# All projection products of a two-layer-kind network as 64x32 tiles

## The chip, the cores and the metric

The kernel runs on one core of one Trainium2 chip. The metric is the time of one execution on the device in microseconds (us), as the median of several runs. The core's engines are TensorE (PE in the profile; its weight loads are listed apart as PEld), VectorE (DVE), ScalarE (ACT), GpSimd (POOL) and SyncE (SP). Each takes its own stream of instructions in order; they wait for one another by semaphores.

## The reference

The input x has 2048 tokens of 448 features in bfloat16. Four layers follow one another, A, B, A, B, each added to x after a layer norm of its input; both A layers have the same weights, and so have both B layers.

```python
def A(x, wqkv, wo):        # 16 heads of 28 features
    q, k, v = split(x @ wqkv)
    idx = pos[:, None] - 2 * arange(8)[None, :]      # 8 keys, 2 tokens apart
    logits = einsum("bhsd,bhswd->bhsw", q, k[idx]) * 28 ** -0.5   # masked where idx < 0
    o = einsum("bhsw,bhswd->bhsd", softmax(logits), v[idx])
    return o @ wo

def B(x, w_gate, w_up, w_down):                      # inner size 1792
    return ((x @ w_gate) * (x @ w_up)) @ w_down
...
x = x + A(layernorm(x), A_wqkv, A_wo)
x = x + B(layernorm(x), B_w_gate, B_w_up, B_w_down)
x = x + A(layernorm(x), A_wqkv, A_wo)
x = x + B(layernorm(x), B_w_gate, B_w_up, B_w_down)
```

The matrix products with a weight (queries, keys, values, `wo`, gate, up, down) are called projections below. The two einsums of A are the score products and the value products.

## The kernel before

**Storage.** x stays in SBUF for the whole kernel (`x_sb`). Each layer norm writes normalised blocks of 128 tokens (`xn_sb`), which are transposed into `xnTa` (for A) or `xnTb` (for B), by the DMA queues or, for the first chunks, by TensorE with an identity (line 660). 448 features are 7 times 64, so all projections contract over 64 rows at a time.

**Projections.** Two products of 64 rows and 128 output columns make a pair: one stands on rows 0 to 63 of the array, the other on rows 64 to 127, and they write different PSUM banks. This tile mode is `MAIN = "R64"`. There are three places. `twin` (line 698) computes queries and keys, or the values of two blocks of queries, in 7 pairs, of which 3 come before a crossing and 4 after. At the crossing the two row halves change places: a bank that was written from the upper rows is now written from the lower ones, and TensorE waits for a semaphore of its own earlier products. `twin_blocks` (line 714) computes the product with `wo` and the product with `w_down` for two blocks of 128 tokens, with such a crossing in the middle; the splitting at crossings is made by `crossed`. `b_chunk` (line 983) computes gate (rows 0 to 63) and up (rows 64 to 127), 7 pairs for 128 of the 1792 inner columns, up to 512 tokens long. ScalarE copies gate out of PSUM (line 989), VectorE multiplies it with up (line 992).

**Attention.** Queries are taken in blocks of 120 (128 for the first), two blocks to a group. `attn_front` makes 64 score products of 28 rows by 64 columns (line 862, mode `R32`, placed by `tile_position`), ScalarE exponentiates them (line 869), VectorE masks them (line 879). `attn_back` makes 64 value products of 64 rows by 32 columns (line 896, mode `C32`): eight tiles, two row halves by four strips of 32 columns. Their result is copied into the ring `O_sb` of four slots (lines 910 and 914) and normalised by `norm` (lines 924 to 937). 17 groups' worth of such work, 1088 score and 1088 value products, lie in the two A layers. The last blocks of the last B layer use full-height products of 128 by 128 (line 1004, mode `F`, as are the warm-up of line 565 and the transposes).

**What sets the order.** The kernel writes its instructions into a planner first (`Sched`). Every task has a duration, dependencies, a priority (from its place in `SEQ`, plus the tables `PR` by kind and `JP` by chunk) and, on TensorE, a tile mode; the planner simulates the engines, adds a cost where TensorE changes its mode (`SWITCH`), hands out the 8 PSUM banks (`A_CAP` and `B_CAP` limit what A and B tasks hold while the other waits), and holds tasks of another mode back for a while to collect them (`HOLD_A`, `HOLD_N`). A task of the mode `MAIN` is taken without such holding. The order that comes out is emitted as fixed instruction streams, with semaphore waits where a task depends on another engine. In the estimate of a TensorE task, `n = 2 * len(ins)` is its number of instructions, since every product brings its own weight load:

```python
n = 2 * len(op.ins)
credit = min(self.CREDIT, credit + (now - clast) / self.FETCH)
if n > 40:
    est = max(est, (n - credit) * self.FETCH + (self.HICCUP if n > credit + 40 else 0.0))
```

Of the kernel before, what the change touches and what calls it, by code (L numbers as in the profile page):

```python
# [9 lines left out]
S = 2048  # L10
D = 448
H = 16
# [12 lines left out]
FC = F // 128  # L25
ACT_TABLE_SET = 6

MAIN = "R64"
PE_T = ("00", "01", "02", "03", "04")
HEAD_LN = 5  # L30
HEAD_P = (-53.71, -30.23, -20.33, -12.94, -19.33)
HOLD_A = 1000.0
HOLD_BA = 2000.0
HOLD_BB = 500.0
# [1 line left out]
S_EST = 270.0  # L36
VX = 120.0
# [5 lines left out]
VT = 4  # L43
NV2 = 6
NXN_ = 6
NO = 4
# [2 lines left out]
AVC = True  # L49
AVC_E = ("act", "dve")  # L50
NBK = 8
PR = {'AV': 8.84, 'rstd': -5.66, 'bn': 0.73, 'N': -2.82, 'Gps': -1.08, 'Tps': 16.85, 'H': 18.16, 'S': 10.61, 'VT': 19.61, 'Ex': 16.77, 'G': -2.93, 'xn': -6.19, 'QK': -6.56, 'Ddps': -26.52, 'V': 22.93, 'x': -0.84, 'lnv': -15.5, 'Oc': -6.51, 'Oa': -6.47, 'R': -19.3, 'VVps': 1.22, 'Yps': -25.3, 'PW': 58.69, 'T': -9.57, 'mv': 2.02, 'Rs': -2.57, 'Rl': 21.52, 'QKps': 4.71, 'E': -7.15, 'wqk': -9.31, 'wqp': -11.53}
JP = {'A20': -3.02, 'B32': 16.28, 'B34': 16.21, 'A22': 20.13, 'B13': 2.73, 'A21': 6.27, 'B12': -2.81, 'A02': -0.21, 'A03': 4.03, 'B30': 4.3, 'B31': 8.23, 'B10': 21.86, 'B11': -14.15, 'A23': 29.86, 'A04': -0.79, 'B33': 153.62, 'A01': -5.33, 'B14': 4.53, 'A00': -24.6}
XL = (2300.0, 2200.0, 4200.0, 5000.0, 5500.0)
WVL = 5000.0
STL = (2400.0, 2600.0, 2900.0, 2800.0)
# [8 lines left out]
FILL = 30  # L65
SEED = 190
JITTER = 0
ATT_P = 1.96
A_CAP = 4
B_CAP = 8  # L70
SEQ = "A00 A01 B10 A02 B11 A03 A04 B12 A20 B13 A21 B14 B30 A22 B31 A23 B32 B33 B34".split()


# [38 lines left out]

class Op:
    __slots__ = ("engs", "ins", "est", "deps", "mode", "prio", "acquire", "release", "idx", "eng",
                 "dma", "lat", "after", "start", "end", "seen", "selfd", "tmin")

    def __init__(self, **kw):
        for k in self.__slots__:
# [11 lines left out]
class Sched:  # L130
# [87 lines left out]
    def schedule(self):  # L218
# [5 lines left out]
        mode = None  # L224
        credit, clast = self.CREDIT, 0.0
        ndep, users = {}, {}
        pend = {e: [] for e in self.ENGS}
# [4 lines left out]
        for op in self.ops:  # L232
            srcs = set()
            for k in op.deps:
                src = self.ready[k][0]
                srcs |= {src.idx} if src.dma is None else {o.idx for o in self.dgroup[(src.dma, src.mode)]}
            if op.after is not None:
                srcs.add(op.after.idx)
            ndep[op.idx] = len(srcs)
            for s in srcs:  # L240
                users.setdefault(s, []).append(op)
            if not srcs:
                for e in op.engs:
                    pend[e].append(op)
        left = len(self.ops)
        now = 0.0
        while left:
            moved = False
            b_ready = any(o.acquire is not None and o.acquire.kind == 1 for o in pend["pe"])
            for e in self.ENGS:  # L250
# [2 lines left out]
                best = None  # L253
                cands = []
                for op in pend[e]:
                    r = self.ready_at(op, e)
                    if r <= now + 1e-6:
                        cands.append((op.prio, op.idx, op))
                cands.sort()
                a_wait = False  # L260
# [1 line left out]
                for *_, op in cands:  # L262
                    if op.acquire is not None:
# [4 lines left out]
                        kind = op.acquire.kind  # L268
# [32 lines left out]
                op = best  # L301
# [13 lines left out]
                if e == "pe":  # L315
                    if mode is not None and op.mode != mode:
                        est += self.SWITCH
                    mode = op.mode
                    n = 2 * len(op.ins)
                    credit = min(self.CREDIT, credit + (now - clast) / self.FETCH)  # L320
                    if n > 40:
                        est = max(est, (n - credit) * self.FETCH + (self.HICCUP if n > credit + 40 else 0.0))
                    credit = max(0.0, credit + est / self.FETCH - n)
                    clast = now + est
                op.start, op.end = now, now + est
# [12 lines left out]
                for u in users.get(op.idx, ()):  # L338
                    ndep[u.idx] -= 1
                    if ndep[u.idx] == 0:  # L340
                        for x in u.engs:
                            pend[x].append(u)
            if moved:
# [2 lines left out]
            for e in self.ENGS:  # L346
                if not pend[e]:
                    continue
                if free[e] > now + 1e-6:
                    c = [free[e]]  # L350
                else:
                    c = [self.ready_at(op, e) for op in pend[e]]
                    c += [f + self.LAT for f in self.free_at]
                c = [t for t in c if t > now + 1e-6]
                if c and (nxt is None or min(c) < nxt):
                    nxt = min(c)
# [65 lines left out]

def pe_cols(n):
    return n / 2.4 + 2.6


def act_est(n, psum=True):
# [11 lines left out]
def build(nc, A_x, A_wqkv, A_wo, B_w_gate, B_w_up, B_w_down, out):  # L439
# [42 lines left out]
    sc = Sched()  # L482
# [122 lines left out]
    def ring(n, freekey):  # L605
        i = rpos[n] % len(rings[n])
        rpos[n] += 1
        prev = rings[n][i]
        rings[n][i] = freekey
        return i, prev  # L610
# [63 lines left out]
    def crossed(parts, deps, prio, est, acquire, kind):  # L674
        prev, prevk = None, []
        prio += PR.get(kind, 0.0)
        for n, (half, ins, pdeps) in enumerate(parts):
            cross = n > 0 and half != parts[n - 1][0]
            if n + 1 < len(parts) and parts[n + 1][0] != half:
                xid[0] += 1  # L680
                tags = [("cross", xid[0], h) for h in (0, 1)]
                ins = ins[:-2] + [(fn, [t] + ([k] if k is not None else [])) for (fn, k), t in zip(ins[-2:], tags)]
                nextk = tags
            else:
                nextk = []
            prev = sc.add("pe", ins, len(ins) / 2 * est + (VX if kind == "VVps" else 0.0), deps=deps + pdeps, mode=MAIN, prio=prio, acquire=acquire if n == 0 else None,
                          after=prev, selfd=prevk if cross else ())
            prevk = nextk
        return prev

    def twin(u, tdeps, prio):
        seen, last = set(), {w: (s, h) for s, sl in enumerate(SLOTS) for h, (w, c, lo) in enumerate(sl)}
        parts = [(0, [], []), (1, [], [])]
        for s, sl in enumerate(SLOTS):
            for h, (w, c, lo) in enumerate(sl):
                st, sp_ = w not in seen, last[w] == (s, h)
                seen.add(w)
                parts[0 if s < 3 else 1][1].append((lambda E, w=w, c=c, lo=lo, st=st, sp_=sp_: E.matmul(  # L698
                    u["out"](w), u["lhs"](w, c, lo, lo + 64), u["rhs"](w, c, lo, lo + 64), start=st, stop=sp_), u["keys"][w] if sp_ else None))
        crossed(parts, u["deps"] + tdeps, prio, pe_cols(u["n"]), u["bk"], u["kind"])  # L700

    def twin_blocks(outs, lhs, rhs, keys, groups, gdeps, deps, prio, acquire):
        first, last = groups[0][0], groups[-1][-1]
        parts = []
        for flip in (0, 1):
            for g, chunks in enumerate(groups):
                ins = []
                for c in chunks:
                    for h in (0, 1):
                        w = h ^ flip  # L710
                        st = c == first and flip == 0
                        sp_ = c == last and flip == 1
                        lo = 64 * h
                        ins.append((lambda E, w=w, c=c, lo=lo, st=st, sp_=sp_: E.matmul(outs(w), lhs(w, c, lo), rhs(w, c, lo), start=st, stop=sp_), keys[w] if sp_ else None))  # L714
                parts.append((flip, ins, gdeps[g]))
        crossed(parts, deps, prio, pe_cols(D), acquire, keys[0][0] + "ps")

# [169 lines left out]
    def attn_back(li, g, slot, prio):  # L887
        qbs, nc = grp_qbs(g), grp_nc(g)
        nd = len(qbs)
        bk = Banks(2, pair=True)  # L890
        ins = []
        for hc, d, c, b in [(hc, d, c, b) for hc in range(4) for d in range(nd) for c in range(2) for b in range(4)]:
            h, o, q = 4 * hc + b, (hc * nd + d) * nc, (li, qbs[d])
# [2 lines left out]
            ins.append((lambda E, b=b, c=c, o=o, vw=vw: E.matmul(ps[32 * b:32 * b + 32, bk[c], o:o + nc], vw, E_sb[64 * c:64 * c + 64, slot, b, o:o + nc],  # L896
                                                               start=True, stop=True, tile_position=(64 * c, 32 * b)), None))
        ins[-1] = (ins[-1][0], [("AV", li, q) for q in qbs])
        sc.add("pe", ins, S_EST * nd / 2, deps=[("E", li, g, 0), ("E", li, g, 1), "c_v"] + [(k, li, q) for k in ("V", "VT") for q in qbs], mode="C32", acquire=bk, prio=prio)
        while nd == 2 and rpos["o"] % NO == NO - 1:  # L900
            rpos["o"] += 1
        oring = [ring("o", ("N", li, q)) for q in qbs]
        o0, nq = oring[0][0], qb_info(qbs[0])[3]
        assert nd == 1 or oring[1][0] == o0 + 1
        O = O_sb[:, o0:o0 + nd, 0:4 * nq].rearrange("p d (h n) -> p d h n", h=4)
# [57 lines left out]
    def b_chunk(li, j, n_b, prio):  # L963
# [15 lines left out]
        for m in range(FC):  # L979
            u, ins = us[m], []  # L980
            for k in range(7):
                for w in range(2):
                    ins.append((lambda E, u=u, k=k, w=w: E.matmul(u["out"](w), WGU[64 * w:64 * w + 64, k, 128 * u["fc"]:128 * u["fc"] + 128],  # L983
                                                                 X[64 * w:64 * w + 64, k, c0:c0 + nt], start=k == 0, stop=k == 6), u["keys"][w] if k == 6 else None))
            sc.add("pe", ins, 7 * pe_cols(nt), deps=u["deps"] + tdeps, mode=MAIN, prio=prio, acquire=u["bk"])
            for u in us[m:m + 1]:
                bk, fc = u["bk"], u["fc"]
# [147 lines left out]
```

## Time and profile before

| what | value |
|---|---|
| median of 3 runs | 393.48 us (393.34 to 393.48) |
| span of the profiled execution | 391.9 us |
| around the span (median less span) | 1.6 us |
| instructions in the trace | 13,910 |
| DMA, mean over the span | 57 GB/s |
| DMA in the first three fortieths of the span | 275, 295 and 306 GB/s |

The span runs from the first to the last instruction of the profiled execution; its own time outside the profiler is not listed, so the median stands for it. The page gives busy time by engine, busy tenths in 40 slices, DMA queues, the chain of work that ended last, and the costliest groups of instructions with their mean duration and the idle time before them. [...] The queues of kind "instruction" bring the engines' own instruction streams; the others move data. "issue" as the end of an idle time means that the engine waited for nothing that the profile shows.

### The profile page before, as it was taken

How to read it: one execution, taken by the hardware profiler on the slowest of the kernel's cores; microseconds unless marked ns; L12 is line 12 of the kernel's file. 1: busy time of each engine (PE TensorE's matmuls, PEld its weight loads, DVE VectorE, ACT ScalarE, POOL GpSimd, SP SyncE). 2: the span in 40 equal slices, each digit the busy share in tenths (PEclk: the TensorE clock that was granted, in tenths of full speed). 3: DMA queues.
4: the chain of work that ended last, by engine and by line, in shares of the span. 5: the costliest groups of instructions: out<-in, count | busy, mean ns of one | idle time of the engine just before them, and what ended most of it. 6: DMA issues, size and time to landing. Idle time of an engine off the chain costs nothing.

```text
span 391.9 us, 13910 instructions
## 1 busy us (share of the span) xinstructions
PE 384.9 (98%) x6142; PEld 213.8 (55%) x6142; DVE 271.2 (69%) x596; ACT 207.3 (53%) x398; POOL 7.6 (2%) x36
## 2 busy tenths in 40 slices
PE   8999999999999999999999999999999999999997
PEld 6655657545444544554546867444454544444674
DVE  6989899669967765684788645258942689477252
ACT  4888876478523745467651523268315782263230
POOL 6010000000000000000000000000000000000000
DMA  8990161501220401320121141010050102403101
GB/s 275 295 306 19 24 93 28 106 13 30 48 49 15 80 15 35 64 28 15 17 49 21 36 95 29 25 20 11 12 128 7 26 7 47 95 4 16 34 27 47
DMA packets 54703, 22.47 MB, mean 57 GB/s; under 512 B 44836, under 2 KB 54644, under 8 KB 54644
## 3 DMA queue, kind: packets, MB, share of 16 engines
q1 hardware_dynamic: 53284, 19.47, 23.7%
q10 hardware_dynamic: 1360, 2.12, 1.8%
q8 instruction: 48, 0.79, 0.8%
q14 instruction: 11, 0.09, 0.1%
HBM read 8.54 MB, written 2.71 MB: 29 GB/s over the span
## 4 chain that ended last, share of the span: by engine, by line
PE 90%; DVE 4%; DMA 2%; ACT 2%; issue 1%; SPq 0%; DVEq 0%
PE ps L983 41%; PE ps L714 25%; PE ps L698 16%; PE ps L896 3%; PE ps L862 3%; PE ps L1004 1%; DMA xnTb<-xn_sb 1%; DMA x_sb<-in_A_x_dram 1%; PE ps L660 1%; DVE xn_sb L651 1%; DVE st L630 1%; DVE x_sb L954 1%; ACT R_sb L925 1%; ACT R_sb L926 1%; DVE E_sb L879 0%
## 5 line engine op out<-in xcount | busy, mean ns | idle before, releaser
L983 PE MATMUL ps<-xnTb,WGU 64*128 64x512 bf16 (+1 forms) x1960 | 180.5, 333 | 0.9 <-DMA xnTb<-xn_sb 0.9
L983 PEld LDWEIGHTS ps<-xnTb,WGU 64*128 64x128 bf16 x1960 | 93.5, 94 | 73.8 <-ACT g_sb L989 1.5
L989 ACT ACTIVATE g_sb<-ps 128x512 bf16<-128x512 f32 (+1 forms) x140 | 71.4, 511 | 95.0 <-PE ps L983 94.3
L992 DVE TENSOR_TENSOR hT<-g_sb,ps 128x512 bf16<-128x512 bf16 (+1 forms) x140 | 79.3, 574 | 55.1 <-ACT g_sb L989 46.1
L714 PE MATMUL ps<-WD,hT 64*128 64x448 bf16 x840 | 84.0, 349 | 0.1
L714 PEld LDWEIGHTS ps<-WD,hT 64*128 64x128 bf16 x840 | 40.2, 94 | 37.0 <-DVE hT L992 0.8
L698 PE MATMUL ps<-xnTa,WQK 64*128 64x512 bf16 (+1 forms) x504 | 53.5, 353 | 0.3
L954 DVE TENSOR_TENSOR x_sb<-x_sb,ps 128x448 bf16<-128x448 bf16 x62 | 36.2, 614 | 24.9 <-PE ps L714 24.8
L630 DVE BATCH_NORM_STATS2 st<-x_sb 128x6 f32<-128x448 bf16 x64 | 37.5, 615 | 2.7 <-DMA x_sb<-in_A_x_dram 2.7
L869 ACT ACTIVATE E_sb<-ps 128x1024 bf16<-128x1024 f32 (+1 forms) x36 | 33.5, 980 | 9.6 <-PE ps L862 9.3
L750 ACT ACTIVATE qk<-ps 128x1024 bf16<-128x1024 f32 (+1 forms) x30 | 27.1, 921 | 19.3 <-PE ps L698 19.0
L651 DVE TENSOR_SCALAR xn_sb<-x_sb,mv,rstd 128x512 bf16<-128x512 bf16 (+1 forms) x64 | 33.7, 569 | 4.7 <-ACT rstd L635 4.5
L698 PEld LDWEIGHTS ps<-xnTa,WQK 64*128 64x128 bf16 x504 | 23.5, 94 | 24.0 <-ACT xnTa L666 0.8
L879 DVE TENSOR_TENSOR E_sb<-E_sb,MK 128x1024 bf16<-128x1024 bf16 (+2 forms) x40 | 23.9, 613 | 8.8 <-ACT E_sb L869 8.5
L714 PE MATMUL ps<-wo_g,oT 64*128 64x448 bf16 x256 | 29.1, 349 | 0.0
L633 ACT ACTIVATE lnv<-mv,eps_sb 128x2 f32<-128x2 f32 (+1 forms) x33 | 9.5, 293 | 30.4 <-DVE mv L632 30.2
L937 DVE TENSOR_TENSOR oT<-O_sb,R_sb 128x480 bf16<-128x480 f32 (+3 forms) x36 | 22.1, 627 | 3.4 <-ACT R_sb L926 3.1
L925 ACT ACTIVATE R_sb<-R_sb 128x480 f32<-128x480 f32 (+1 forms) x34 | 20.1, 600 | 5.6 <-DVE R_sb L924 5.6
L924 DVE STREAM_SHUFFLE R_sb<-O_sb 128x480 f32<-128x480 f32 (+1 forms) x34 | 22.7, 696 | 0.0
L698 PE MATMUL ps<-WV,xnTa 64*128 64x336 bf16 (+3 forms) x252 | 22.2, 304 | 0.2
L926 ACT ACTIVATE R_sb<-R_sb 128x480 f32<-128x480 f32 (+1 forms) x34 | 20.1, 602 | 0.4
L714 PEld LDWEIGHTS ps<-wo_g,oT 64*128 64x128 bf16 x256 | 12.3, 94 | 11.6 <-DVE oT L937 0.4
(47 smaller groups left out, 170.7 us busy)
## 6 DMA issues: line engine op xcount, KB each, us to landing
out_dram<-x_sb SPq DMA_DIRECT2D x15, 112.0 KB, 1.7
WD<-in_B_w_down_dram SPq DMA_DIRECT2D x2, 784.0 KB, 11.5
WGU<-in_B_w_up_dram SPq DMA_DIRECT2D x2, 784.0 KB, 17.6
WGU<-in_B_w_gate_dram ACTq DMA_DIRECT2D x2, 784.0 KB, 13.3
x_sb<-in_A_x_dram SPq DMA_DIRECT2D x3, 448.0 KB, 6.4
vt<-qk SPq DMA_DIRECT2D x42, 16.0 KB
xnTb<-xn_sb SPq DMA_TRANSPOSE x32, 3.0
x_sb<-in_A_x_dram SPq DMA_DIRECT2D x2, 224.0 KB, 4.2
```

The costliest lines, as they stand in the source:

```text
L630: sc.add("dve", one(lambda E, B=B: E.bn_stats(st6[:, B, :], x_sb[:, B, :]), ("bn", li, B)), 525.0, deps=[("x", li - 1, B)] + ([("xn", li - ...
L651: sc.add("dve", one(lambda E, B=B, dst=dst, src=src: E.tensor_scalar(dst, src, mv[:, B, 0:1], rstd[:, B:B + 1], ALU.subtract, ALU.mult), ( ...
L698: parts[0 if s < 3 else 1][1].append((lambda E, w=w, c=c, lo=lo, st=st, sp_=sp_: E.matmul(u["out"](w), u["lhs"](w, c, lo, lo + 64), u["rhs ...
L714: ins.append((lambda E, w=w, c=c, lo=lo, st=st, sp_=sp_: E.matmul(outs(w), lhs(w, c, lo), rhs(w, c, lo), start=st, stop=sp_), keys[w] if s ...
L750: return E.activation(dst, src, ACT.Copy) if hasattr(E, "activation") else E.tensor_copy(dst, src)
L869: return E.activation(E_sb[:, slot, 2 * hp:2 * hp + 2, 0:w], ps[:, b0:b0 + 2, 0:w], ACT.Exp, scale=SCALE)
L925: sc.add("act", one(lambda E: E.activation(R_sb[:, rs, 0:w], R_sb[:, rs, 0:w], ACT.Ln), ("Rl", li, qb)), act_est(w, False), deps=[("Rs", l ...
L926: sc.add("act", one(lambda E: E.activation(R_sb[:, rs, 0:w], R_sb[:, rs, 0:w], ACT.Exp, scale=-1.0), ("R", li, qb)), act_est(w, False), de ...
L954: sc.add("dve", one(lambda E: E.tensor_tensor(x_sb[:, B, :], x_sb[:, B, :], ps[:, bk[w], 0:D], ALU.add), ("x", li, B)), dve_est(D), deps=[ ...
L983: ins.append((lambda E, u=u, k=k, w=w: E.matmul(u["out"](w), WGU[64 * w:64 * w + 64, k, 128 * u["fc"]:128 * u["fc"] + 128], X[64 * w:64 * ...
L989: sc.add("act", one(lambda E, gs=gs, bk=bk: E.activation(g_sb[:, gs, 0:nt], ps[:, bk[0], 0:nt], ACT.Copy), ("G", li, j, fc)), act_est(nt), ...
L992: sc.add("dve", one(lambda E, gs=gs, bk=bk, fc=fc: E.tensor_tensor(hT[:, fc, hs, 0:nt], g_sb[:, gs, 0:nt], ps[:, bk[1], 0:nt], ALU.mult), ...
```

## The change

Every projection product of 64 by 128 is written as four products of 64 by 32, one on each strip of 32 array columns, by a new helper:

```diff
-MAIN = "R64"
+MAIN = "C32"
...
-ATT_P = 1.96
+ATT_P = 1.0
 A_CAP = 4
-B_CAP = 8
+B_CAP = 6
...
+def strips(out, lhs, rhs, start, stop, row, key=None):
+
+    def strip(s):
+        return lambda E: E.matmul(out()[32 * s:32 * s + 32], lhs()[:, 32 * s:32 * s + 32], rhs(), start=start, stop=stop, tile_position=(row, 32 * s))
+    return [(strip(s), key if s == 3 else None) for s in range(4)]
```

`twin`, `twin_blocks` and `b_chunk` call it in place of one `E.matmul` each, with `row` 0 or 64:

```diff
-                    ins.append((lambda E, u=u, k=k, w=w: E.matmul(u["out"](w), WGU[64 * w:64 * w + 64, k, 128 * u["fc"]:128 * u["fc"] + 128],
-                                                                 X[64 * w:64 * w + 64, k, c0:c0 + nt], start=k == 0, stop=k == 6), u["keys"][w] if k == 6 else None))
+                    ins += strips(lambda u=u, w=w: u["out"](w), lambda u=u, k=k, w=w: WGU[64 * w:64 * w + 64, k, 128 * u["fc"]:128 * u["fc"] + 128],
+                                  lambda k=k, w=w: X[64 * w:64 * w + 64, k, c0:c0 + nt], k == 0, k == 6, 64 * w, u["keys"][w] if k == 6 else None)
```

So the mode of the projections is that of the value products, and the planner treats the value products as `MAIN` too. The task durations in the planner stay what they were (`len(ins) / 8 * est` in place of `len(ins) / 2 * est`). At a crossing the second half waits for the last product of the first half alone, where there were two tags. In `attn_back` the value products themselves now wait for a free slot of `O_sb`, where only the copies did:

```diff
-        sc.add("pe", ins, S_EST * nd / 2, deps=[("E", li, g, 0), ("E", li, g, 1), "c_v"] + [(k, li, q) for k in ("V", "VT") for q in qbs], mode="C32", acquire=bk, prio=prio)
+        sc.add("pe", ins, S_EST * nd / 2, deps=[("E", li, g, 0), ("E", li, g, 1), "c_v"] + [(k, li, q) for k in ("V", "VT") for q in qbs] + [r[1] for r in oring], mode=MAIN, acquire=bk, prio=prio)
```

The planner's estimate for a task with many instructions becomes

```diff
-                    if n > 40:
-                        est = max(est, (n - credit) * self.FETCH + (self.HICCUP if n > credit + 40 else 0.0))
+                    fetch = (n - credit) * self.FETCH
+                    if fetch > est:
+                        est = fetch + (self.HICCUP if n > credit + 100 else 0.0)
```

The tables `PR`, `JP` and `HEAD_P` have new values, so the order on every engine is another; the rest of the planner's edits (`rdy`) keep a value that was computed anew each time. TensorE's products are 6142 before and 17,578 after.

More of the change, by code (lines that the diff above doesn't have):

```diff
@@ L26 @@
 ACT_TABLE_SET = 6
-MAIN = "R64"
+MAIN = "C32"
 PE_T = ("00", "01", "02", "03", "04")
 HEAD_LN = 5
-HEAD_P = (-53.71, -30.23, -20.33, -12.94, -19.33)
+HEAD_P = (-60.1, -28.46, -20.04, -19.66, -19.03)
 HOLD_A = 1000.0
@@ L51 @@
 NBK = 8
-PR = {'AV': 8.84, 'rstd': -5.66, 'bn': 0.73, 'N': -2.82, 'Gps': -1.08, 'Tps': 16.85, 'H': 18.16, 'S': 10.61, 'VT': 19.61, 'Ex': 16.77, 'G': -2.93, 'xn': -6.19, 'QK': -6.56, 'Ddps': -26.52, 'V': 22.93, 'x': -0.84, 'lnv': -15.5, 'Oc': -6.51, 'Oa': -6.47, 'R': -19.3, 'VVps': 1.22, 'Yps': -25.3, 'PW': 58.69, 'T': -9.57, 'mv': 2.02, 'Rs': -2.57, 'Rl': 21.52, 'QKps': 4.71, 'E': -7.15, 'wqk': -9.31, 'wqp': -11.53}
-JP = {'A20': -3.02, 'B32': 16.28, 'B34': 16.21, 'A22': 20.13, 'B13': 2.73, 'A21': 6.27, 'B12': -2.81, 'A02': -0.21, 'A03': 4.03, 'B30': 4.3, 'B31': 8.23, 'B10': 21.86, 'B11': -14.15, 'A23': 29.86, 'A04': -0.79, 'B33': 153.62, 'A01': -5.33, 'B14': 4.53, 'A00': -24.6}
+PR = {'AV': -76.5, 'rstd': 11.09, 'bn': 0.91, 'N': 7.02, 'Gps': -1.64, 'Tps': 7.27, 'H': -12.07, 'S': 4.41, 'VT': -10.04, 'Ex': 17.97, 'G': 87.98, 'xn': -12.63, 'QK': 3.17, 'Ddps': -20.99, 'V': 31.96, 'x': -0.65, 'lnv': -11.9, 'Oc': -7.3, 'Oa': -5.3, 'R': -21.09, 'VVps': 2.07, 'Yps': -57.58, 'PW': 44.14, 'T': -2.37, 'mv': -4.13, 'Rs': -11.6, 'Rl': 26.4, 'QKps': 4.71, 'E': -5.63, 'wqk': -9.37, 'wqp': -8.95}
+JP = {'A20': -39.71, 'B32': 34.27, 'B34': -54.93, 'A22': 20.53, 'B13': 4.2, 'A21': 15.6, 'B12': -0.24, 'A02': 1.24, 'A03': 9.63, 'B30': 6.56, 'B31': 7.4, 'B10': -7.36, 'B11': -26.26, 'A23': 30.63, 'A04': -58.23, 'B33': 7.56, 'A01': -4.1, 'B14': 3.5, 'A00': -14.21}
 XL = (2300.0, 2200.0, 4200.0, 5000.0, 5500.0)
@@ L114 @@
     __slots__ = ("engs", "ins", "est", "deps", "mode", "prio", "acquire", "release", "idx", "eng",
-                 "dma", "lat", "after", "start", "end", "seen", "selfd", "tmin")
+                 "dma", "lat", "after", "start", "end", "seen", "selfd", "tmin", "rdy")
     def __init__(self, **kw):
@@ L242, in schedule @@
             if not srcs:
+                op.rdy = {x: self.ready_at(op, x) for x in op.engs}
                 for e in op.engs:
@@ L255, in schedule @@
                 for op in pend[e]:
-                    r = self.ready_at(op, e)
-                    if r <= now + 1e-6:
+                    if op.rdy[e] <= now + 1e-6:
                         cands.append((op.prio, op.idx, op))
@@ L340, in schedule @@
                     if ndep[u.idx] == 0:
+                        u.rdy = {x: self.ready_at(u, x) for x in u.engs}
                         for x in u.engs:
@@ L351, in schedule @@
                 else:
-                    c = [self.ready_at(op, e) for op in pend[e]]
+                    c = [op.rdy[e] for op in pend[e]]
                     c += [f + self.LAT for f in self.free_at]
@@ L680, in crossed @@
                 xid[0] += 1
-                tags = [("cross", xid[0], h) for h in (0, 1)]
-                ins = ins[:-2] + [(fn, [t] + ([k] if k is not None else [])) for (fn, k), t in zip(ins[-2:], tags)]
-                nextk = tags
+                tag = ("cross", xid[0])
+                fn, k = ins[-1]
+                ins = ins[:-1] + [(fn, [tag] + ([k] if k is not None else []))]
+                nextk = [tag]
             else:
                 nextk = []
-            prev = sc.add("pe", ins, len(ins) / 2 * est + (VX if kind == "VVps" else 0.0), deps=deps + pdeps, mode=MAIN, prio=prio, acquire=acquire if n == 0 else None,
+            prev = sc.add("pe", ins, len(ins) / 8 * est + (VX if kind == "VVps" else 0.0), deps=deps + pdeps, mode=MAIN, prio=prio, acquire=acquire if n == 0 else None,
                           after=prev, selfd=prevk if cross else ())
@@ L697, in twin @@
                 seen.add(w)
-                parts[0 if s < 3 else 1][1].append((lambda E, w=w, c=c, lo=lo, st=st, sp_=sp_: E.matmul(
-                    u["out"](w), u["lhs"](w, c, lo, lo + 64), u["rhs"](w, c, lo, lo + 64), start=st, stop=sp_), u["keys"][w] if sp_ else None))
+                parts[0 if s < 3 else 1][1].extend(strips(lambda w=w: u["out"](w), lambda w=w, c=c, lo=lo: u["lhs"](w, c, lo, lo + 64),
+                                                          lambda w=w, c=c, lo=lo: u["rhs"](w, c, lo, lo + 64), st, sp_, lo, u["keys"][w] if sp_ else None))
         crossed(parts, u["deps"] + tdeps, prio, pe_cols(u["n"]), u["bk"], u["kind"])
@@ L713, in twin_blocks @@
                         lo = 64 * h
-                        ins.append((lambda E, w=w, c=c, lo=lo, st=st, sp_=sp_: E.matmul(outs(w), lhs(w, c, lo), rhs(w, c, lo), start=st, stop=sp_), keys[w] if sp_ else None))
+                        ins += strips(lambda w=w: outs(w), lambda w=w, c=c, lo=lo: lhs(w, c, lo), lambda w=w, c=c, lo=lo: rhs(w, c, lo), st, sp_, lo, keys[w] if sp_ else None)
                 parts.append((flip, ins, gdeps[g]))
@@ L890, in attn_back @@
         bk = Banks(2, pair=True)
+        while nd == 2 and rpos["o"] % NO == NO - 1:
+            rpos["o"] += 1
+        oring = [ring("o", ("N", li, q)) for q in qbs]
         ins = []
@@ L898, in attn_back @@
         ins[-1] = (ins[-1][0], [("AV", li, q) for q in qbs])
-        sc.add("pe", ins, S_EST * nd / 2, deps=[("E", li, g, 0), ("E", li, g, 1), "c_v"] + [(k, li, q) for k in ("V", "VT") for q in qbs], mode="C32", acquire=bk, prio=prio)
-        while nd == 2 and rpos["o"] % NO == NO - 1:
-            rpos["o"] += 1
-        oring = [ring("o", ("N", li, q)) for q in qbs]
+        sc.add("pe", ins, S_EST * nd / 2, deps=[("E", li, g, 0), ("E", li, g, 1), "c_v"] + [(k, li, q) for k in ("V", "VT") for q in qbs] + [r[1] for r in oring], mode=MAIN, acquire=bk, prio=prio)
         o0, nq = oring[0][0], qb_info(qbs[0])[3]
```

## The prediction

> **What bounds the kernel now.** I read the page's first section, then the chain of waits, then the costliest groups. The profiled execution has a span of 391.9 us; the median of the timed runs is 393.48, so 1.6 us lie around the span and are added at the end.
>
> ```profile
> span 391.9 us, 13910 instructions
> ...
> PE 384.9 (98%) x6142; PEld 213.8 (55%) x6142; DVE 271.2 (69%) x596; ACT 207.3 (53%) x398; POOL 7.6 (2%) x36
> ...
> q8 instruction: 48, 0.79, 0.8%
> ...
> PE 90%; DVE 4%; DMA 2%; ACT 2%; issue 1%; SPq 0%; DVEq 0%
> ...
> L983 PE MATMUL ps<-xnTb,WGU 64*128 64x512 bf16 (+1 forms) x1960 | 180.5, 333 | 0.9 <-DMA xnTb<-xn_sb 0.9
> ```
>
> TensorE is the bound: 98% busy, 90% of the chain. Its work is projection products in pairs, one on rows 0-63 and one on rows 64-127, which run side by side. In the chain 14 such products of 512 columns (7 pairs) take 1.51 us, 216 ns a pair. The third line is the one to keep: q8 is the queue that brings TensorE's instructions, 0.79 MB in 48 refills of 16 KB. TensorE has 12,422 records in the trace (6142 products, 6142 weight loads, 138 waits and the like), 259 for each refill; the stalls below make it 256.
>
> **The array time of a projection does not change.** A pair becomes eight products of 64x32. Attention's value products (line 896) already run in this tile mode, so the trace shows what eight strips do. In the first 0.1 us of the run at 82.45 us, the instructions had piled up ahead of the array, and eight products of 64 columns start every 29 ns (single starts at 82.489, 82.518, 82.547): 64 columns at the full clock (26.7) plus 2.4 ns. The same rule gives 216 ns at 512 columns, what a pair takes now. That the four strips do not run at once is thereby excluded. Nor do weight loads show: the load for the first strip's third product started at 82.502 while its second ran from 82.489. [...]
>
> **What it removes.** I counted mode changes in the two orders of TensorE's instructions: 75 before, 54 after, 21 fewer (value products join the projections; score products, transposes and the last full-height products still switch).
>
> ```profile
> 82.45 0.68 PE L896 MATMUL ps<-E_sb,v_sb 64*32 64x64 bf16 x64
> 83.06 1.69 PE L983 MATMUL ps<-xnTb,WGU 64*128 64x512 bf16 x14
> 84.68 0.71 PE L862 MATMUL ps<-qk 28*64 28x64 bf16 x64
> ...
> 86.78 0.54 PE L896 MATMUL ps<-E_sb,v_sb 64*32 64x64 bf16 x47
> 88.09 0.26 PE L896 MATMUL ps<-E_sb,v_sb 64*32 64x64 bf16 x17 [0.78 <-issue]
> ```
>
> The 14 products from 83.06 take to 84.68, 1.62 us against 1.51 undisturbed: 0.11 for a switch, and other switches lie at 0.09 to 0.11. 21 x 0.10 = 2.1 us off. The second tag of a row crossing is dropped as well; its wait has other work in front of it, so I count nothing.
>
> **What it adds: instructions.** Lines 983, 714 and 698 hold 1960 + 840 + 256 + 504 + 252 = 3812 products. They become 15,248, each with its own weight load: 2 x 11,436 = 22,872 instructions more, 35,294 in all, 22,872 / 256 = 89 refills more, 137 in all. Issue alone has room: in the steady part of line 896 one instruction takes 4.2 ns (8.3 ns a product), so the 16 of an eight-strip group need 67 ns, under the 72 to 216 ns that the group occupies the array. The question is whether the refills keep up.
>
> **What a refill costs.** The last two rows above are a stall: 47 products, nothing from 87.12 to 88.09, then 17. No semaphore ends it; the profile writes "issue". There are two more, at 31.45 (0.15 us) and here:
>
> ```profile
> 266.72 1.34 PE L896 MATMUL ps<-E_sb,v_sb 64*32 64x64 bf16 x126
> 268.24 0.20 PE L896 MATMUL ps<-E_sb,v_sb 64*32 64x64 bf16 x2 [0.17 <-issue]
> ```
>
> Their positions give the cause. Counts of products and weight loads up to just inside each stall:
>
> ```profile
> 0.00:31.50 31.50, 29.01 (x473) 18.03 (x473) 25.73 (x73) 22.90 (x50) 7.62 (x36) 1.00 0.94 278
> 0.00:87.50 87.50, 83.69 (x1741) 51.40 (x1741) 73.55 (x183) 62.46 (x124) 7.62 (x36) 1.00 0.52 130
> 0.00:268.00 268.00, 263.61 (x4528) 149.29 (x4529) 196.56 (x448) 155.92 (x302) 7.62 (x36) 1.00 0.30 67
> ```
>
> With the 15, 39 and 96 other records these are 961, 3521 and 9153 instructions: 2560 and 5632 apart, 10 and 22 times 256 exactly. So each stall stands at a refill boundary. By the trace's packet records the last refill before each was number 3 (28.99 to 30.21 us), 13 (85.64 to 86.70) and 35 (265.82 to 266.90), again 10 and 22 apart. TensorE went on 1.39, 1.39 and 1.34 us after the packet's end. And the next refill was not asked for until then: it started 1.69, 1.99 and 1.34 us after TensorE went on, and took 0.95 us each time. So one refill is in flight at a time, a boundary is not passed until the one before has landed, and the full turn is request + packet + delivery:
> 1.69 + 0.95 + 1.36 = 4.0; 1.99 + 0.95 + 1.36 = 4.3; 1.34 + 0.95 + 1.36 = 3.64 us. Mean 3.98 us for 256 instructions, 15.5 ns each.
>
> Now, 256 instructions last 391.9 / 48 = 8.2 us on average, so only bursts meet that limit. After the change the array wants 256 of them in 16 groups: 3.45 us at 512 columns, 3.0 at 448, 1.75 at 256. Over all projections the array time is 588 x 215.8 + 392 x 109.2 (line 983), 548 x 189.2 (714) and 66.6 (698), 340 us, for 30,496 instructions: 2.85 us per 256. Every kind is under 3.98. So TensorE starves at nearly every boundary, and refills become the bound through the whole kernel.
>
> [...]
>
> **The sum.** TensorE starts projecting at 9.5 us as before and passes the first boundary soon after. The first refills lie in the stretch full of loads: before, number 1 ran 15.46 to 16.59, delivered 17.9; number 3 started 3.6 us after its boundary, so a turn there is 3.6 + 1.2 + 1.36 = 6.2. Refills 2 and 3 land at 24.1 and 30.3, 4 at 34.3 (a turn of 4.0). Then 132 turns to number 136: 132 x 3.98 = 525.4. The last 285 instructions hold the full-height products, slower than a refill:
>
> ```profile
> 381.24 2.75 PE ps L1004 x14
> 383.99 2.76 PE ps L714 x28
> 386.75 2.80 PE ps L1004 x28
> ```
>
> 8.3 us, and 2.35 from there to the end of the span. 34.3 + 525.4 + 8.3 + 2.35 = 570.4, with 1.6 around it **572 us**.
>
> Everything else hides beneath: the 2.1 us of switches, the new order's priorities and bank caps, and the wait that value products now make for a free slot of O_sb (behind it on TensorE's queue stand the next projections, which starve anyway; without that cover it is late by at most one normalisation step, about 0.6 us in rows 924 to 937, 18 times). VectorE and ScalarE, 271 and 207 us busy, get slack.
>
> The unknown is the turn under steady starving. From below: the shortest request that can be read with no stall, about 0.96 us (refill 34, started 259.21, its boundary passed near 258.25), packet 0.95, delivery 1.24 (refill 2, 24.24 to 25.48): 3.15, which gives 462. From above, 1.99 + 1.25 + 1.39 = 4.63: 658. Both ends need the extreme of three terms at once, 133 times; I take the mean of the three turns seen whole, and 475 to 630 as the range (3.25 to 4.4).
>
> **Rivals.**
> - *Refills do not bind* (faster). The buffer holds more blocks than I read, and the three stalls were a late request only. Then the switches count: 393.5 - 2.1, with one long stall (0.97) perhaps gone, **390 to 391.5**. For it: most boundaries in the trace pass without a gap. Against it: those were 5 us and more apart, but for those bursts. It decides if TensorE passes two boundaries within 3 us in a row without stopping.
> - *Two refills in flight.* A block every 2 us: only 256-column stretches starve, (392 + 56) groups x 16 / 256 = 28 blocks x 0.25 = 7, less 2: **398**. Against it: no request went out during the stall of 0.97 us.
> - *Weight loads show* in long columns, 14 ns (load 82.475 to product 82.489) on each of 1906 groups: 27 us, **418**, refills hidden. Against it: the burst above.
>
> **Chances.** Forecast 0.86, refills not binding 0.08, two in flight 0.03, weight loads 0.03. About 0.2% (0.8 us) is what a measurement of this kernel can tell from no change; of the first rival 0.01 falls inside. Faster 0.07, same 0.01, slower 0.92. The range 475 to 630 holds nearly all of the forecast's 0.86, some 0.8.
>
> **What would show it.** In the profile after: q8 with about 137 refills; TensorE's busy share well below 98%, about 60 to 75%, with idle before lines of projections put down to "issue"; stops every 256 instructions and refills 3.6 to 4.3 us apart; groups of eight still 216 ns apart between stops; 54 mode changes. Wrong would be: refills closer than 3 us, or groups slower than 216 ns. If the idle time also lowered the granted clock (1.00 in every window here), it would be slower still.

## The result, and the profile after

The changed kernel takes 550.47 us (three runs, 549.35 to 552.98) where the kernel before takes 393.48: a ratio of 1.4005, 95% interval 1.3944 to 1.4065. The forecast was 572 with a range of 475 to 630. The profiled execution has a span of 551.2 us and took 552.98.

From the page of the changed kernel (sections 1 to 5; PEclk is the granted TensorE clock in tenths for 40 equal slices):

```profile
span 551.2 us, 36763 instructions
...
PE 423.3 (77%) x17578; PEld 267.4 (49%) x17578; DVE 282.8 (51%) x606; ACT 204.4 (37%) x390; POOL 6.8 (1%) x34
...
PEclk9669899999999999999999899999999999999998
...
q8 instruction: 138, 2.26, 1.8%
...
PE 76%; issue 22%; POOL 1%; ACT 1%; DVE 0%; POOLq 0%
...
L432 PE MATMUL ps<-xnTb,WGU 64*32 64x512 bf16 (+1 forms) x7840 | 204.3, 338 | 62.6 <-issue 60.9
```

TensorE falls from 98% busy to 77%, and what replaces it in the chain is not another engine but "issue", from 1% to 22%: TensorE waits for nothing that the profile shows. The instruction queue q8 brings 138 refills in place of 48. The last line is gate and up: 62.6 us of idle time in front of its products, 60.9 of them "issue", where line 983 had 0.9 in all.

The timeline of TensorE in the changed kernel, in a stretch of gate and up at 256 columns (start, length, what, and the idle time before):

```profile
308.29 2.84 PE L432 MATMUL ps<-xnTb,WGU 64*32 64x256 bf16 x128 [2.12 <-issue]
311.76 2.31 PE L432 MATMUL ps<-xnTb,WGU 64*32 64x256 bf16 x127 [0.63 <-issue]
315.65 1.94 PE L432 MATMUL ps<-xnTb,WGU 64*32 64x256 bf16 x128 [1.58 <-issue]
319.00 1.26 PE L432 MATMUL ps<-xnTb,WGU 64*32 64x256 bf16 x73 [1.41 <-issue]
```

This is the whole result in four lines. 128 products with their weight loads are 256 instructions; TensorE does them in 2 to 3 us, stops, and starts again 3.47, 3.89 and 3.35 us after the start before. The second line has one product fewer; waits are instructions of the same stream and count too (the one remainder of 193 below comes out only with them).

Over the whole trace I took the refill packets and the positions in TensorE's stream. A boundary is the place behind a block of 256 instructions; a stop is the time from the last start before it to the first start behind it. Of the 137 boundaries, 129 have a stop of 0.25 us or more, 163.8 us in all. Every one of the 129 stands at a position that leaves 193 when it is divided by 256, as the three stops of the kernel before do (961, 3521, 9153). The span grew by 159.3 us, so the stops account for the loss; the 4.5 us between the two sums were not taken apart. After each stop TensorE goes on 1.2 to 1.7 us after the end of a refill packet, 1.39 on average. No two refills start less than 3.2 us apart. Between the stops a group of eight strips follows the last at 216 ns for 512 columns, 189 for 448 and 109 for 256 (medians, from start to start; a strip of 512 columns is listed with 377 ns, so listed durations overlap), exactly as a pair did.

### The profile page after: what moved, and what is told of

It is laid out like the page before. It is cut to its first block, busy times and chain, and to the rows that moved or that the text cites. A ratio compares the mean times of both kernels' runs of the same rounds, so it can differ in the third digit from the quotient of the medians.

```text
span 551.2 us, 36763 instructions
## 1 busy us (share of the span) xinstructions
PE 423.3 (77%) x17578; PEld 267.4 (49%) x17578; DVE 282.8 (51%) x606; ACT 204.4 (37%) x390; POOL 6.8 (1%) x34
## 4 chain that ended last, share of the span: by engine, by line
PE 76%; issue 22%; POOL 1%; ACT 1%; DVE 0%; POOLq 0%
PE ps L432 69%; PE ps L872 2%; PE ps L909 2%; PE ps L1014 1%; PE ps L669 1%; POOL hT L554 1%; PE ps L574 0%; ACT qk L760 0%; ACT g_sb L999 0%; POOL MK L558 0%; DVE WQK L582 0%; ACT R_sb L936 0%; POOL WQK L545 0%; ACT O_sb L920 0%; DVE hT L1002 0%
## 5 line engine op out<-in xcount | busy, mean ns | idle before, releaser
L432 PE MATMUL ps<-xnTb,WGU 64*32 64x512 bf16 (+1 forms) x7840 | 204.3, 338 | 62.6 <-issue 60.9
L432 PEld LDWEIGHTS ps<-xnTb,WGU 64*32 64x32 bf16 x7840 | 117.9, 93 | 129.9 <-issue 86.9
L432 PE MATMUL ps<-WD,hT 64*32 64x448 bf16 x3360 | 91.7, 352 | 13.3 <-issue 13.3
L432 PEld LDWEIGHTS ps<-WD,hT 64*32 64x32 bf16 x3360 | 52.6, 93 | 43.7 <-issue 21.4
L432 PE MATMUL ps<-xnTa,WQK 64*32 64x512 bf16 (+1 forms) x2016 | 64.4, 371 | 10.8 <-issue 10.5
L432 PEld LDWEIGHTS ps<-xnTa,WQK 64*32 64x32 bf16 x2016 | 32.6, 96 | 30.8 <-issue 16.5
L432 PE MATMUL ps<-WV,xnTa 64*32 64x336 bf16 (+3 forms) x1008 | 29.6, 321 | 17.5 <-issue 17.5
L879 ACT ACTIVATE E_sb<-ps 128x1024 bf16<-128x1024 f32 (+1 forms) x36 | 33.5, 979 | 23.9 <-PE ps L872 23.8
L760 ACT ACTIVATE qk<-ps 128x1024 bf16<-128x1024 f32 (+1 forms) x26 | 24.5, 941 | 38.8 <-PE ps L432 38.7
L432 PE MATMUL ps<-wo_g,oT 64*32 64x448 bf16 x1024 | 32.2, 354 | 4.4 <-issue 4.4
L889 DVE TENSOR_TENSOR E_sb<-E_sb,MK 128x1024 bf16<-128x1024 bf16 (+2 forms) x40 | 23.9, 612 | 18.3 <-ACT E_sb L879 17.9
L432 PEld LDWEIGHTS ps<-WV,xnTa 64*32 64x32 bf16 x1008 | 16.5, 94 | 24.5 <-issue 21.5
L432 PEld LDWEIGHTS ps<-wo_g,oT 64*32 64x32 bf16 x1024 | 18.0, 94 | 14.3 <-issue 8.0
```

The source lines that it names most:

```text
L432: return lambda E: E.matmul(out()[32 * s:32 * s + 32], lhs()[:, 32 * s:32 * s + 32], rhs(), start=start, stop=stop, tile_position=(row, 32 ...
L760: return E.activation(dst, src, ACT.Copy) if hasattr(E, "activation") else E.tensor_copy(dst, src)
L879: return E.activation(E_sb[:, slot, 2 * hp:2 * hp + 2, 0:w], ps[:, b0:b0 + 2, 0:w], ACT.Exp, scale=SCALE)
L889: return E.tensor_tensor(e, e, m, ALU.mult)
```

## The experiments

Theory: TensorE's instructions arrive in blocks of 256, one refill in flight, some 3.9 us a turn in the changed kernel (3.80 by the fuller count further down); a stretch that uses 256 faster stops at each boundary. Rivals: column strips are slow in themselves; every added instruction has a price (157 us over 22,872 is 6.9 ns); the new order has a part.

All kernels but the last keep one of the two orders on every engine and change only what is emitted for each projection product, so the planner's choices do not enter.

**Null products, three for each product.** The first try at instructions without strips.

```diff
+def product(E, out, lhs, rhs, start, stop, row):
+    def null():
+        for _ in range(3):
+            E.matmul(out[:, 0:8], ZERO[0][row:row + 64, :], rhs[:, 0:8], start=False, stop=False)
+    if not start:
+        null()
+    i = E.matmul(out, lhs, rhs, start=start, stop=stop)
+    if start:
+        null()
+    return i
```

> The kernel before, its order and its 64x128 pairs kept; each projection product has three null products of 8 columns (zero weights, same rows, same bank, adding nothing) beside it. So TensorE has as many instructions as the changed kernel, 35,294, but no column strips. Refill theory (256 instructions at a time, one refill in flight, 3.88 us a turn in the changed kernel): 540 to 570 us, some 137 refills, nearly every boundary a stop. Rival, the column strips themselves are slow: the null products cost the array 3 x 5.8 = 18 ns a pair on 1906 pairs, 34 us, so about 428 us.

Measured: 583.31 us, ratio 1.4837 (1.4748 to 1.4926). Above both expectations, and inconclusive as a test: only 41 of 137 boundaries stop, 42 us in all. The rest is array time that I had priced wrongly, as the next run shows.

**Null products, one for each product** (the same with `range(1)`).

> As with three null products, but one beside each projection product: 20,046 instructions, 78 refills. Refill theory has a threshold: 256 instructions now last 7.1 us at 512 columns, 6.2 at 448 and 4.7 at 336, above the turn of 3.9, and 3.7 only at 256 columns; so 393.5 + 11 (array time of the nulls) + 3 (256-column stretches) + a few bursts = 403 to 415 us. Rival, a price for each instruction (157 us for 22,872, 6.9 ns): 393.5 + 11 + 52 = 457 us.

Measured: 444.65 us, ratio 1.1304 (1.1278 to 1.1331), between the two. The timeline of this kernel says why:

```profile
229.97 0.17 PE L433 MATMUL ps<-WD,zero 64*128 64x8 bf16 x2
230.00 0.35 PE L436 MATMUL ps<-WD,hT 64*128 64x448 bf16 x2
230.19 0.17 PE L433 MATMUL ps<-WD,zero 64*128 64x8 bf16 x2
230.21 0.35 PE L436 MATMUL ps<-WD,hT 64*128 64x448 bf16 x2
230.40 0.17 PE L433 MATMUL ps<-WD,zero 64*128 64x8 bf16 x2
230.43 0.35 PE L436 MATMUL ps<-WD,hT 64*128 64x448 bf16 x2
```

A pair of 448 columns with its null pair comes every 215 ns where the pair alone took 189: a null pair costs about 26 ns, not 6. Nothing idles there; "issue" is 1% of the chain. No run isolates why, but the pieces of the next experiment show the same floor: there five pairs of 33 or 34 columns take 126 ns and five of 44 or 45 take 125 (medians), about 25 ns a pair at either width. 1906 pairs x 25 ns = 48 us, and 6.3 us of stops, 5 more than before: 393.1 + 48 + 5 = 446. With three nulls it is 143 us, so 256 instructions last longer than a turn at 512 columns (16 x (216 + 75) ns = 4.7 us), and 393.1 + 143 + 42 = 578. Both runs fit the refills, but they price the filler and do not separate the theories.

**Five pieces.** Instructions without strips once more, with pieces that I took to be long enough to cover a weight load (an estimate). Where a pair is inside its accumulation (neither first nor last in a bank, nor at a crossing), each product becomes five (`NP`) of a fifth of the moving columns, on the same 64x128 weights.

```diff
+def in_pieces(E, two):
+    ops = [(p.out(), p.lhs(), p.rhs()) for p in two]
+    n = ops[0][2].shape[-1]
+    for k in range(NP):
+        a, z = n * k // NP, n * (k + 1) // NP
+        for out, lhs, rhs in ops:
+            E.matmul(out[:, a:z], lhs, rhs[:, a:z], start=False, stop=False)
```

> The kernel before with its order, no column strips. Inside each unit, every pair that is neither first nor last nor at a crossing is cut into five pairs of a fifth of the moving columns (same weights loaded five times): 1341 pairs cut, 16,870 products, 33,878 instructions, 132 refills. Here the weight loads run beside products of 34 to 103 columns, so they should hide. Refill theory: 520 to 545 us (132 turns of 3.9, less where the uncut pairs give the refills time). Rival, the column strips are slow: 393.5 + 1341 x 4 x 2.5 ns = 407 us, at most 425 if some loads show.

Measured: 528.78 us, ratio 1.3454 (1.3407 to 1.35). From this kernel's page and its waits (line, what it waited for, us in total, times, longest):

```profile
PE 434.2 (82%) x16870; PEld 371.8 (71%) x16870; DVE 274.5 (52%) x596; ACT 209.6 (40%) x398; POOL 7.7 (1%) x36
...
q8 instruction: 132, 2.16, 1.7%
...
PE 81%; issue 17%; DMA 1%; ACT 0%; DVE 0%; SPq 0%; DVEq 0%
```

```profile
PE ps L452 <- issue: 64.4, 62, 4.5
PE ps L924 <- issue: 11.2, 7, 3.9
```

No projection uses a column strip here, yet the same signature stands: 17% "issue", 86 of 131 boundaries stop, 105.0 us in all. "Column strips are slow" gave 407 to 425 and is out. The pieces also cost array time: a pair in five pieces takes 237, 210 and 132 ns at 512, 448 and 256 columns (medians), about 21 ns more than the pair where the expectation had 10, some 29 us over 1341 pairs. With the stops that is the loss of 136 us to within 4. A price of 6.9 ns for each instruction would come near as well (21,456 more: 541 us); the next two runs decide on it.

**Two strips of 64 columns** (64x64 tiles, the order of before).

```diff
+def product(E, out, lhs, rhs, start, stop, row):
+    for s in range(0, 128, 64):
+        i = E.matmul(out[s:s + 64], lhs[:, s:s + 64], rhs, start=start, stop=stop, tile_position=(row, s))
+    return i
```

> The kernel before and its order, each projection product as two strips of 64 columns (64x64 tiles); 20,046 instructions. Refill theory: 256 instructions last 6.9 us at 512 columns and 3.5 at 256, so 393.5 + about 14 blocks x 0.4 + a few bursts = 395 to 408 us. Rival, column strips are slow, in part by their number: a third to a half of the loss, 445 to 470 us. Rival, a price for each instruction: 446 us.

Measured: 404.0 us, ratio 1.0267 (1.0239 to 1.0295), inside the refill theory's 395 to 408. The waits of TensorE in this kernel:

```profile
PE ps L868 <- issue: 4.2, 3, 2.3
PE ps L429 <- DMA xnTb<-xn_sb: 1.6, 1, 1.6
...
PE ps L429 <- issue: 0.8, 1, 0.8
```

7,624 instructions more cost 10.9 us, not 52: there is a threshold, not a price per instruction. Seven stops of 0.25 us or more remain, 6.8 us in all, most of it in front of score products (line 868). They are 5.5 us more than before; the other 5 us were not traced.

**Four strips in the product with `w_down` alone** (the same helper with strips of 32, called where `keys[0][0] == "Dd"`).

> The kernel before with its order, four strips in the product with w_down alone: 5040 instructions more, in 26 stretches, with up to 52 more mode changes (5 us). Refill theory: only the second and later boundaries of a stretch stop, some 6720 / 256 - 15 = 11 stops of 0.9 us, so 402 to 412 us. Rival, a price of 6.9 ns for each instruction: 393.5 + 35 + 5 = 433 us.

Measured: 406.27 us, ratio 1.0346 (1.0313 to 1.0379), inside 402 to 412. Thirteen stops, 11.1 us, against eleven of 0.9 expected. A part of its timeline where nothing stops:

```profile
205.62 0.92 PE L720 MATMUL ps<-wo_g,oT 64*128 64x448 bf16 x8
206.47 1.52 PE L429 MATMUL ps<-WD,hT 64*32 64x448 bf16 x56
207.92 1.69 PE L720 MATMUL ps<-wo_g,oT 64*128 64x448 bf16 x16
209.53 1.52 PE L429 MATMUL ps<-WD,hT 64*32 64x448 bf16 x56
210.99 0.93 PE L720 MATMUL ps<-wo_g,oT 64*128 64x448 bf16 x8
```

56 strips, seven groups, start at 206.47 and are followed at 207.92: 1.45 us, with a mode change at either end, where seven undisturbed groups take 1.32. So the very products that starve in the changed kernel run at full speed when the stretch is short (112 instructions) and sparse work surrounds it. A price per instruction gave 433.

**Strips with the old order.** Each 64x128 product of the kernel before is emitted as four strips of 64x32.

> The kernel before with its order on every engine, but each 64x128 product is emitted as four strips of 64x32: the strips without the new order. Refill theory: 137 refills at the changed kernel's mean turn, 540 to 565 us, within 2% of the changed kernel. Rival, order and strips share the loss: clearly below, 480 to 530 us.

Measured: 543.51 us, ratio 1.384 (1.3795 to 1.3886), inside 540 to 565; 113 of its 137 boundaries stop, 146 us in all.

**Pairs with the new order:** the changed kernel emits each group of four strips as the one product that it was.

```diff
     def strip(s):
-        return lambda E: E.matmul(out()[32 * s:32 * s + 32], lhs()[:, 32 * s:32 * s + 32], rhs(), start=start, stop=stop, tile_position=(row, 32 * s))
+        return lambda E: E.matmul(out(), lhs(), rhs(), start=start, stop=stop) if s == 3 else None
```

> The changed kernel with its new order on every engine, but each group of four strips is emitted as the one 64x128 product that it was. Refill theory: the loss is in the strips' instructions alone, so 388 to 400 us; the order itself moves little. Rival, the new order has a part in the loss: well above 400 us.

Measured: 395.02 us, ratio 1.0035 (1.0022 to 1.0048), inside 388 to 400. The strips alone make a ratio of 1.38, the order alone 1.0035; the order has next to no part. With strips the new order is even about 1% worse than the old one (1.4005 against 1.384).

**A planner that knows of refills.** A try at something better than both: the planner counts TensorE's instructions (`icount`), keeps the time in ns at which each block of 256 has landed (`landed`), and lengthens a task that needs a block earlier. The heart of the edit:

```diff
+                    late, first = 0.0, icount
+                    icount += n
+                    for b in range(first // 256 + 1, icount // 256 + 1):
+                        t = now + late + est * (256 * b - first) / n
+                        late += max(0.0, landed[b] - t)
+                        landed[b + 1] = max(t - 400.0, landed[b]) + 3500.0
+                    est += late
```

> A try at a better version: the kernel before, pairs kept; only the planner is told of refills (a block of 256 instructions lands 3.5 us after the boundary before it was passed, and a TensorE task that needs it earlier is longer by the wait), so its order shifts around the bursts of score and value products. There are 1.5 us of stops to gain; 391.5 to 395 us, and as likely no gain as one.

Measured: 395.7 us, ratio 1.0073 (1.0046 to 1.0101): above the 391.5 to 395 expected, and 0.7% slower than before. Its two stops at boundaries of 0.25 us or more sum to 0.95 us, against 1.3 before, and the new order loses more than that elsewhere; where was not traced. Nothing here beats the kernel before.

## Why the prediction was right, and where it was off

*The bound.* It was read from three stops of 1.5 us together in a trace where TensorE was 98% busy. Their positions, 10 and 22 x 256 instructions apart, and the 1.34 to 1.39 us after a packet's end held: 129 stops in the changed kernel follow the same rule, 1.39 us on average. The sign named for the first rival, two boundaries within 3 us without a stop, did appear once: products go on without a stop at 45.06 and at 47.95 us, 2.89 us apart. It does not speak for that rival. TensorE had waited 0.6 us for ScalarE just before the first (`ACT qk L760`), and the two refills behind these boundaries had started 5.6 us apart (39.31 and 44.96) and landed 4.4 and 1.8 us before they were needed. So the sign can appear where TensorE comes late to the first boundary, and decides nothing by itself.

*The array time.* 216, 189 and 109 ns a group between stops, as read from 0.1 us of the value products; 216 less 109 for 256 columns is 0.42 ns a column, which is the prediction's 26.7 ns for 64. Weight loads that show, the third rival, would have lengthened the groups; they did not. The 64x32 loads of the projections are listed with 93 to 96 ns (means by group), the 64x128 loads of the kernel before with 94.

*The counts.* 137 refills forecast, 138 seen; 54 mode changes forecast and seen; 75% to 60% busy forecast, 77% seen, just outside.

*The turn.* This is the mis-sized term. Forecast 3.98 us: 1.67 request, 0.95 packet, 1.36 delivery, from three turns. Measured, after the head, over 123 turns between two stops: 1.28 + 1.13 + 1.39 = 3.80 us. The request was too long by 0.39: three samples from 1.34 to 1.99 us were too few, and one of them lay in the head; the packet was too short by 0.18, so about half of the error cancelled by luck. From the landing of refill 3 to that of refill 135 the forecast has 4.0 + 131 x 3.98 = 525.4 us, the trace 503.0 (33.5 to 536.5): 22.4 us less. Refill 3 itself landed at 33.5 for 30.3, 3.2 us more, and from refill 135 to the end of the span the trace has 14.7 us for 14.6. So the span is 19 us shorter than forecast; the other 2.3 us of the difference are that the median lies 0.7 us below this execution's span, where 1.6 above was assumed.

*The head.* The turns there were put at 6.2 us; the first two took 8.9 and 8.7 (6.0 and 5.7 us of it from TensorE's restart to the packet), in a stretch where the DMA engines are fully busy (share 1.00 from 0 to 28 us). That is 5.2 us more than forecast; the first refill had landed earlier, at 15.9 for 17.9, which makes up for 2.0 of it. The prediction named a lower clock as a risk, and it came: from 33.5 to 54.7 us the granted clock was 0.86, and five blocks took 21.2 us where five turns of 3.80 make 19.0.

*The savings.* 2.1 us for the mode changes cannot be seen beneath the stops, nor can the wait of the value products for `O_sb`.

*The first rival.* At 44 of the 47 boundaries of the kernel before, the 256 instructions in front last longer than the 3.8 us of a turn, and only one of the 44 has a stop (0.15 us at 31.45, in the head). Of the other three, two have a stop (at 87.1 and 267.9 us); the third, at 194.6 us, comes 2.54 us after the boundary before it and has none, and there the packet of the last refill had ended at 192.51, 2.1 us earlier. In the changed kernel 129 of 137 boundaries have a stop, of 163.8 / 129 = 1.3 us on average. These stops fit two blocks of 256, one in work and one on its way (an inference from their positions and the packets' times). A larger store that single refills keep full does not fit: in the kernel before, refills start 7.4 us apart (median) though a turn takes 3.8, so there was time to fill it, and TensorE still stopped at 87.1 and 267.9 us. Whether the store is smaller, or a refill is only asked for at a boundary, these runs do not separate.

## What to carry to other kernels

Count instructions per microsecond on each engine as you count bytes: here TensorE could be fed 256 instructions (128 products with their weight loads) each 3.8 us, so a product had to occupy about 30 ns of array time on average, and four strips in place of one product leave less than that (216 / 8 = 27 ns at 512 columns, 14 at 256). Read it from the instruction queue's packets and from idle time that the profile calls "issue", and look whether such stops are whole multiples of one number apart. Short dense bursts cost little here where sparse work surrounded them (seven groups of strips took 1.45 us where seven undisturbed ones take 1.32), so look how long the dense stretches are before giving up small tiles altogether.

## What the runs showed of the hardware beyond this

- The granted clock fell where TensorE was starved longest: the second and third of the 40 slices (14 to 41 us) show 0.6, with stops of 4.4, 5.2 and 3.2 us in the first 34 us; the kernel before has 1.00. The later stops, 2.6 us at most, leave it at 0.97 to 1.00 (windows of 100 us from 200 to 500).
- A pair of 8-column products with 64x128 weights in front of a long pair costs some 25 ns of array time, where the prediction's 2.4 ns a product on top of the columns would make about 6 (an estimate: 8 x 0.42 + 2.4). Pairs of 33 to 45 columns, each with its own weight load, cost 25 ns too (the kernel of five pieces).
- From TensorE's restart to the next refill packet it takes 1.3 us in the body of the changed kernel, and 6.0 and 5.7 us while the DMA engines are full with the first loads (share 1.00 from 0 to 28 us).
